# Attention with a token mixer: in the ending, the values of two steps are multiplied in one burst

## The chip, the cores and the metric

The kernel runs on one core of a Trainium2 chip. The time is the device time of that core in microseconds, the median of several runs. The engines are TensorE (PE in the profile; PEld is its loading of weights, PEq its sequencer), VectorE (DVE), ScalarE (ACT), GpSimd (POOL) and SyncE (SP), which issues most of the DMAs; each works through its own instructions in order. PSUM is the memory that PE writes: eight banks of 128 x 512 float32.

## The reference

Cut to what matters; x is 2048 tokens of 512 channels, and the sizes are 32 heads of 16 and a mixer of width 1792.

```python
xn = layernorm(x)
qkv = xn @ wqkv                                   # 32 heads of 16
p = softmax(einsum("qd,kd->qk", q, k) * 16 ** -0.5)
s = concat_heads(einsum("qk,kd->qd", p, v)) @ wo
h = layernorm(xn)
u = gelu(einsum("sd,sf->df", h, w1) + b1)
g = silu(einsum("df,fs->sd", u, w2) + b2)         # with the axes put back
return x + s * g
```

## The kernel before

**Steps.** After norms and projections, attention goes by pairs of heads: 16 pairs, each in 32 steps, 512 in all. A step t is one pair of heads, one span of 1024 queries and one block of 128 keys: 16 steps (key blocks) for the first span of a pair, 16 for the second. In a step `score` (L961) makes four tiles of scores, for two heads (a = 0, 1) and two halves of the queries. Each is a matmul of 50 rows, on the upper half of the PE array for a = 0 and on the lower for a = 1, so that the two can run side by side; ScalarE's exponential (L973) turns each into a tile `prob`.

`values` (L975) multiplies the four `prob` tiles of a step with the values of its 128 keys: four matmuls (L984), each 128 rows high and 32 columns wide, side by side, summed over the 16 steps of a span in one PSUM tile `av`. The pool of that tile has one bank. At the first step of a span `values` takes a new tile there. At the last step it puts `put_away` (L709) on the list `soon`, which copies `av` out; `run_later` (L507) records what is on that list. The code records instructions in Python's order and every engine gets its own in that order, with semaphores from the tile framework: a new tile in a bank waits until the old tile's last reader is done, also where that reader is recorded later on another engine.

**The main loop** (L1200) takes s = 0, 2, ..., 534 and treats two steps a turn. Up to s = 510 it also computes the row maxima for the steps 22 ahead (L525, L529). From s = 512 (`NU`) none are left; this is the ending. There t = s - 22, and the turn makes the scores of t (i = 0) and t + 1 (i = 1). Per i:

- `a_half` (L1145) records the four scores, interleaved with half-height matmuls of the output product (L1161). Products come from the generator `rest` (L1002 to L1030), three per block of 128 tokens; each is cut into an upper and a lower half. The upper halves are recorded at once, the lower ones two calls later (`second_rows`). With the lower halves the block is complete, and `finish` (L942) is recorded: VectorE multiplies by the gate (L944), adds (L945), SyncE stores the rows (L947), and `load_out` (L931) issues the loads for the third block after it (L938, L940). For s below 524 only i = 0 takes products, from 524 on both do. I call the matmuls of one call a series, and number the blocks 0 to 13 in the order of `blocks` (tokens' blocks 8 to 13, then 0 to 7); tokens' block 0 is number 6.
- one entry of `asides` is recorded, if there is one: `one` (L816: PE transposes L821, VectorE's reciprocals L824 and a copy L826) and `move_in` (L851: matmuls L835, L841, L842, L94, and four DMAs L98). They treat the first span of the last pair of heads, which ends with step 495; its copy is L714. Products of tokens' block 0 and after wait for `move_in`, by `own_done`, four calls of `run_later` later.
- `values` of the steps that are due.

**PSUM.** Before the ending four banks are for scores and sums of products, three for maxima, one for `av`. At s = 512 the seven become one rotation (L1211), from which scores, product blocks (for as long as they are summed) and the asides take tiles in turn.

**After the loop** eight loads of gates (`load_gates`, L956, on POOL's queue; six are recorded at s = 532, two behind the loop) go to buffers of `prob` tiles. Behind the last step's `values` (511), `put_away` copies the tile on ScalarE (L716); then follow products of the last two blocks (L1299), `one` and `two` for the second span (L821, L824, L826, L835), and the eight blocks of the second span are multiplied by their gates and stored (L1328, L1332, L1333).

Of the kernel before, what the change touches and what calls it, by code (L numbers as in the profile page):

```python
# [21 lines left out]
def tile_attention_token_mixer(ctx, tc, x, wqkv, wo, w1, b1, w2, b2, out):  # L22
# [484 lines left out]
    def run_later():  # L507
        now, later[:] = soon + later, []
        soon.clear()
        for f in now:  # L510
            f()

    NU = NP * NB * 2
    mxp = {}

    def max_of(u, half, a, pl=ps_mx, nm="mx"):

        p, r = divmod(u // 2, NB)
        c = u % 2 * 2 + half
        if u // 16 not in mxp:  # L520
            mxp[u // 16] = sm.tile([P, 2, 8, NC], F32, name="mxp")
        q, k = qs[p], ks[p]
        o = 64 * a
        ps = pl.tile([P, 512], F32, name=nm)
        nc.tensor.matmul(  # L525
            ps, q[o : o + 48, r * P : (r + 1) * P], k[o : o + 48, c * 512 : (c + 1) * 512],
            start=True, stop=True,
        )
        nc.vector.tensor_reduce(mxp[u // 16][:, a, r % 8, c : c + 1], ps, axis=AX.X, op=OP.max)  # L529
# [272 lines left out]
    def divisions():  # L802

        if undivided and undivided[0] in away and begun_divisions[0] - len(divided) < 2:
            divide(begun_divisions[0], *undivided.pop(0))
            begun_divisions[0] += 1
# [114 lines left out]
    def load_second():  # L921

        b = next((b for b in unkept if b >= PARTS), min(unkept))
        unkept.remove(b)
        i = b - NB // 2
        while not held or len(held) < NB // 8:
            held.append(big.tile([P, S], F32, name="big"))
        ys[b] = held[i // 4][:, i % 4 * 512 : i % 4 * 512 + 512]
        nc.sync.dma_start(ys[b], y_d[b] if b < PARTS else xv[:, b, :])
# [45 lines left out]
    def values(t):  # L975
        p, r = divmod(t, SPP)
        span, kb = divmod(r, NB)
        if kb == 0:
            state["av"] = ps_av.tile([P, 512], F32, name="av")
        av = state["av"]  # L980
        for a in range(2):
            for c in range(2):
                j = 2 * a + c
                nc.tensor.matmul(  # L984
                    av[32 * j : 32 * j + 32, :],
                    vps[p][:, kb, 16 * a : 16 * a + 32], prob.pop((t, a, c)),
                    start=kb == 0, stop=kb == NB - 1,
                )
        if kb == NB - 1:
            soon.append(lambda: put_away(p, span, av))  # L990
# [70 lines left out]
    def take(n, each):  # L1061

        nonlocal open_, done
        got = 0
        while open_ and (got < n or fill.peek() and len(fill.peek()) == 2):
            x = fill.next()
            if x is False:
                open_ = False
            elif x is None:
                break  # L1070
            elif len(x) == 2:
                def then(empty, back):
                    empty()
                    back()

                each(None, lambda x=x: then(*x))
                if fill.peek() is None:
                    fill.next()
                    break
            else:  # L1080
                each(x, None)
                got += 1
        done += got
# [20 lines left out]
    def order(n):  # L1104

        return ORDERS[min(x for x in ORDERS if x >= n)]

    def halves(lead, n):


        parts, then = ([], []), []

        def each(x, f):
            if f:
                then.append(f)
                return
            ps, w, m, first, last = x
            for a, made in ((lead, parts[0]), (1 - lead, parts[1])):
                r = slice(64 * a, 64 * a + 64)
                made.append(lambda r=r, start=first and a == lead, stop=last and a != lead: nc.tensor.matmul(  # L1120
                    ps, w(r), m(r), start=start, stop=stop,
                ))

        take(n, each)
        return *parts, then
# [3 lines left out]
    def count():  # L1129


        left = -done
        for i, n in enumerate(sizes):
            left += n
            if left > 0:
                break
        if left == 9:
            return 4
        return min(6, -(-left // -(-3 * left // (15 if i == SLOW else 16)))) if left > 0 else 0
# [35 lines left out]
    def items(s, a):  # L1175

        mx, sc = [], []
        for i in range(4):
            t = s - LEAD + i // 2
            if s < NU:  # L1180
                mx.append(lambda i=i: max_of(s + i // 2, i % 2, a))
            if 0 <= t < NT:
                sc.append(lambda t=t, i=i, at=(ps_mx, "mx") if a and s >= NU else (ps_sc, "sc"): score(t, i % 2, a, *at))
        return mx, sc
# [8 lines left out]
    def piece():  # L1193
        if pieces:
            pieces.pop(0)()
            return True
        return False

    lead = 0
    for s in range(0, total + 1, 2):  # L1200
        t = s - LEAD
        now[0] = s
        if s >= NU or t < 0:
            run_later()
        if done >= n_fill // 2 + 3 * NF:
            divisions()
        if s >= NU - SPP + LEAD and unkept:
            load_second()
        if s == NU:

            ps_sc.free += ps_mx.free  # L1211
            ps_mx.free = ps_sc.free
        heads = [items(s, a) for a in range(2)]
        if s < NU and t >= 0:
            steady[0] = True
            one, two, then = halves(lead, count())
            made = [dict(D=part, m=heads[a][0], s=heads[a][1]) for part, a in ((one, lead), (two, 1 - lead))]
            first, second, *places = order(len(one))
            if one:
                lead = 1 - lead  # L1220
            for i, kinds in enumerate((*zip(first, second), "")):
                if i in places:

                    if i == places[0]:
                        piece()
                    now[0] = s + places.index(i)
                    if now[0] >= LEAD + 2:
                        values(now[0] - LEAD - 2)
                    run_later()
                for of, kind in zip(made, kinds):  # L1230
                    if of[kind]:
                        of[kind].pop(0)()
            for f in then:
                f()
        elif s < NU:

            for i in range(4):
                for a in range(2):
                    max_of(s + i // 2, i % 2, a, *first_banks[n_max % 4])
                    n_max += 1  # L1240
                end = i == 3 and s + 2 == LEAD
                some = []
                take(EARLY[n_max // 2 % len(EARLY)], lambda *x: some.append(x))
                for x in some:
                    lanes(*x, stop=end and x is some[-1])
                if end:
                    keep_half()
                if i == 1:
                    now[0] = s + 1
                    run_later()  # L1250
        else:


            for i in range(2):

                a_half(*(heads[a][1][2 * i : 2 * i + 2] for a in range(2)), i == 0 or s >= NU + 2 * (PARTS - NB // 2))
                if not piece() and asides and s < total - 2:
                    asides.pop(0)()
                for v in range(t - 2, t + i):
                    if (v, 0, 0) in prob:  # L1260
                        values(v)
                if i == 0:
                    now[0] = s + 1
                    run_later()
            if s == NU + 4:
                load_last_w()
            if s == total - 2:
                load_gates(NB // 2, NB - 2)
            if s == total - 6:
                split_last_w()  # L1270
        if s < NU and s % 16 == 14:
            pieces[:0] = max_rows(s + 1)
        while t < 0 and piece():
            pass
        for v in (t - 2, t - 1):
            if 0 <= v < NT and (v, 0, 0) in prob:
                values(v)
        if 0 <= t < NT:
            p, r = divmod(t, SPP)
            if r == 0 and p + 1 < NP:  # L1280
                if p > 0:
                    load_qk(p + 1)
                load_v(p + 1)
# [101 lines left out]
```

## Time and profile before

| | |
|---|---|
| median of 3 runs | 1630.51 us (1629.91 to 1630.63) |
| span of the profiled execution | 1628.0 us |
| the profiled execution's own time beside its span | not given by the page |
| busy: PE, DVE, ACT, POOL | 1621.3, 1421.3, 1194.1, 564.1 us |
| the ending, 1563.14 to 1610.13 | 46.99 us |
| behind the last values, 1610.13 to 1628.0 | 17.87 us |

The span runs from the first to the last instruction that the profiler recorded; the time measured from outside also holds what lies around it. Busy times overlap. A busy PE is not PE at its peak: the ends of matmuls are modelled. In rows of the timeline stand the start, the duration, the engine, the line, the operation, the tiles (output<-inputs), their sizes and the number of instructions merged into the row; in brackets how long the engine had been idle, and what ended that.

### The profile page before, as it was taken

Reading aid. Unit: us, or ns where it says so; the run is one execution under the profiler, and the core shown is the slowest. Engines: PE = TensorE matmul, PEld = TensorE weight load, DVE = VectorE, ACT = ScalarE, POOL = GpSimd, SP = SyncE. Lnnn points to the kernel's source line nnn. Section 1 sums busy time; section 2 is a strip of 40 time slices with the busy share of each in tenths; the row PEclk is TensorE's granted clock in tenths of the full one; section 3 lists DMA queues with packets and bytes.
Section 4 is the critical chain, followed back from the end, with each engine's and each line's share of the span. In section 5 each row is a group of like instructions: output and inputs, shape, how many; then the busy total and the mean of one; then the engine's idle time right before and its main releaser. Section 6 shows DMA issues by size and latency. Waiting matters only on the chain.

```text
span 1628.0 us, 31317 instructions
## 1 busy us (share of the span) xinstructions
PE 1621.3 (100%) x11956; PEld 881.9 (54%) x11956; DVE 1421.3 (87%) x2497; ACT 1194.1 (73%) x2313; POOL 564.1 (35%) x672
## 2 busy tenths in 40 slices
PE   9999999999999999999999999999999999999998
PEld 8888855544555544545545545445555455454444
DVE  7665999999999999999999999999999999999955
ACT  3333477777777777777877777777777778888885
POOL 1224844342244432342333332322322224632342
PEclk9999999999999999999999999999999999999999
DMA  7468441514142141916151512314151615353356
GB/s 238 181 237 207 113 89 40 95 43 73 41 72 70 33 79 34 247 62 111 38 86 37 95 55 42 74 28 68 37 85 37 112 38 101 118 95 121 110 156 223
DMA packets 151810, 155.60 MB, mean 96 GB/s; under 512 B 51612, under 2 KB 109980, under 8 KB 148588
## 3 DMA queue, kind: packets, MB, share of 16 engines
q1 hardware_dynamic: 146604, 150.75, 38.2%
q0 software_dynamic: 5056, 2.85, 0.7%
q8 instruction: 94, 1.54, 0.4%
q14 instruction: 56, 0.46, 0.1%
HBM read 101.86 MB, written 50.58 MB: 94 GB/s over the span
## 4 chain that ended last, share of the span: by engine, by line
PE 99%; DVE 0%; DMA 0%; ACT 0%; SPq 0%; issue 0%
PE av L984 31%; PE dn L1120 24%; PE sc L968 18%; PE mx L525 13%; PE sc L428 3%; PE mx L428 2%; PE dn L663 2%; PE av L428 1%; PE dn L664 1%; PE sc L101 0%; PE sc L103 0%; PE sc L102 0%; PE dn L1161 0%; PE dn L1299 0%; PE mx L101 0%; PE mx L103 0%
## 5 line engine op out<-in xcount | busy, mean ns | idle before, releaser
L529 DVE TENSOR_REDUCE mxp<-mx 128x1 f32<-128x512 f32 x2026 | 1250.4, 681 | 120.6 <-PE mx L525 94.0
L973 ACT ACTIVATE prob<-sc 128x512 f32<-128x512 f32 x2004 | 1042.3, 606 | 288.9 <-PE sc L968 128.2
L525 PE MATMUL mx<-big 48*128 48x512 f32 x2026 | 764.8, 416 | 0.0
L968 PE MATMUL sc<-big 50*128 50x512 f32 x2004 | 738.1, 411 | 0.1
L984 PE MATMUL av<-prob,vp 128*32 128x512 f32 x4096 | 545.5, 604 | 0.0
L1120 PE MATMUL dn<-hu,wh 64*128 64x512 f32 x1520 | 514.7, 406 | 0.0
L968 PEld LDWEIGHTS sc<-big 50*128 50x128 f32 x2004 | 356.6, 186 | 254.3 <-ACT prob L973 230.2
L525 PEld LDWEIGHTS mx<-big 48*128 48x128 f32 x2026 | 358.2, 185 | 175.1 <-DVE mxp L529 156.9
L1120 PEld LDWEIGHTS dn<-hu,wh 64*128 64x128 f32 x1520 | 271.5, 184 | 74.9 <-issue 49.8
L1120 PE MATMUL dn<-hu,wl 64*128 64x512 f32 x762 | 302.4, 397 | 0.0
L984 PEld LDWEIGHTS av<-prob,vp 128*32 128x32 f32 x4096 | 80.9, 108 | 181.3 <-issue 169.6
L94 POOL TENSOR_TENSOR wl<-raw,wh 128x512 fp32r<-128x512 f32 x124 | 150.8, 1217 | 60.1 <-ACT wh L166 20.5
L1120 PEld LDWEIGHTS dn<-hu,wl 64*128 64x128 f32 x762 | 140.6, 184 | 12.9
L164 POOL CAST wh<-raw 128x512 fp32r<-128x512 f32 x104 | 60.4, 581 | 183.5 <-DMA raw<-in_B_w_dram 77.3
L552 POOL CAST m<-f 16x128 fp32r<-16x128 f32 x32 | 9.0, 280 | 302.1 <-DVE f L541 302.1
L98 POOL DMA_DIRECT2D big<-m x128 | 66.1, 525 | 2.7 <-PE mx L968 2.7
L613 POOL TENSOR_TENSOR sq<-u 128x512 f32<-128x512 f32 x11 | 11.4, 1041 | 132.8 <-ACT u L607 132.7
L700 POOL TENSOR_SCALAR t<-t 128x512 f32<-128x512 f32 x16 | 23.8, 1488 | 95.7 <-ACT t L697 95.7
L1120 PE MATMUL dn<-wh,hu 64*128 64x512 f32 x168 | 55.0, 393 | 0.0
L428 PE MATMUL sc<-xt,big 128*128 128x512 f32 x184 | 44.3, 389 | 0.0
L94 POOL TENSOR_TENSOR hu<-hx,hu 128x512 fp32r<-128x512 f32 x16 | 20.3, 1289 | 66.9 <-ACT hu L271 66.9
L663 PE MATMUL dn<-hu,wh 64*128 64x512 f32 x128 | 42.3, 391 | 0.0
(228 smaller groups left out, 1221.6 us busy)
## 6 DMA issues: line engine op xcount, KB each, us to landing
raw<-in_B_w_dram SPq DMA_DIRECT2D x104, 256.0 KB
big<-k_d SPq DMA_DIRECT2D x96, 128.0 KB
big<-q_d SPq DMA_DIRECT2D x96, 128.0 KB
q_d<-sg SPq DMA_DIRECT2D x16, 512.0 KB
k_d<-sg SPq DMA_DIRECT2D x16, 512.0 KB
num_d<-ev SPq DMA_DIRECT2D x30, 256.0 KB
u_d<-uo SPq DMA_DIRECT2D x14, 512.0 KB
hu<-u_d SPq DMA_DIRECT2D x14, 512.0 KB
```

The lines of the kernel that those rows point to most:

```text
L94: eng.tensor_tensor(out=o, in0=a, in1=b.bitcast(F32), op=OP.subtract)
L98: queue.dma_start(dst.bitcast(F32), src.bitcast(F32))
L164: nc.gpsimd.tensor_copy(whs[n][:, :m, :], raws[n][:, :m, :])
L428: nc.tensor.matmul(ps, w[part][:, kd, m], xt[kd][:, z, :], start=w is wh and z == 0 and kd == 0, stop=w is wl and kd == ND - 1,)
L525: nc.tensor.matmul(ps, q[o : o + 48, r * P : (r + 1) * P], k[o : o + 48, c * 512 : (c + 1) * 512], start=True, stop=True,)
L529: nc.vector.tensor_reduce(mxp[u // 16][:, a, r % 8, c : c + 1], ps, axis=AX.X, op=OP.max)
L663: nc.tensor.matmul(ps, w(slice(0, 64)), m(slice(0, 64)), start=first, stop=last)
L700: nc.gpsimd.tensor_scalar(t, t, 1.0, None, op0=OP.add)
L968: nc.tensor.matmul(ps, ks[p][o : o + 50, kb * P : (kb + 1) * P], qs[p][o : o + 50, at : at + 512], start=True, stop=True,)
L973: nc.scalar.activation(e, ps, AF.Exp, scale=scale)
L984: nc.tensor.matmul(av[32 * j : 32 * j + 32, :], vps[p][:, kb, 16 * a : 16 * a + 32], prob.pop((t, a, c)), start=kb == 0, stop=kb == NB - 1,)
L1120: made.append(lambda r=r, start=first and a == lead, stop=last and a != lead: nc.tensor.matmul(ps, w(r), m(r), start=start, stop=stop,))
```

## The change

In the ending the call of `values` at i = 0 is left out, save at s = 512. What was due there is called at i = 1 of the same turn, whose range covers it already.

```diff
@@ -1256,7 +1256,7 @@
                 a_half(*(heads[a][1][2 * i : 2 * i + 2] for a in range(2)), i == 0 or s >= NU + 2 * (PARTS - NB // 2))
                 if not piece() and asides and s < total - 2:
                     asides.pop(0)()
-                for v in range(t - 2, t + i):
+                for v in range(t - 2, t + i) if i or s == NU else ():
                     if (v, 0, 0) in prob:
                         values(v)
                 if i == 0:
```

Before, the order on PE from s = 514 on is: scores of t, values of t - 1, scores of t + 1, values of t. After, it is: scores of t, scores of t + 1, values of t - 1 and of t. As t is even there, a span's last step (495) and the next span's first (496) fall into one burst; `put_away` of 495 is then recorded after the matmuls of 496, and waits of the framework keep 496 behind the copy. Since `put_away` is recorded a series later, so are the asides that it appends. The last step (511) is multiplied at i = 1 of s = 534 instead of i = 0.

## The prediction

> **What bounds the kernel now.** I read the page first: the span, then the chain that ended last, which is the tensor engine almost alone.
>
> ```profile
> span 1628.0 us, 31317 instructions
> ...
> PE 99%; DVE 0%; DMA 0%; ACT 0%; SPq 0%; issue 0%
> ```
>
> The edit acts only where no maxima are left (s = 514 to 534), so next I read the timeline from 1558 us on, engine by engine. I count pairs of steps by s. Of PE, the columns are start, duration, engine, line, tiles, count; a `values` burst of one step shows as x8, because each of its four matmuls leaves two records.
>
> ```profile
> 1559.63 1.92 PE L984 MATMUL av<-prob,vp 128*32 128x512 f32 x16
> 1561.48 0.49 PE L968 MATMUL sc<-big 50*128 50x512 f32 x1
> ...
> 1563.14 0.49 PE L968 MATMUL sc<-big 50*128 50x512 f32 x1
> 1563.48 0.39 PE L968 MATMUL sc<-big 50*128 50x512 f32 x1
> 1563.71 0.40 PE L1161 MATMUL dn<-wh,hu 64*128 64x512 f32 x2
> ...
> 1564.50 1.06 PE L984 MATMUL av<-prob,vp 128*32 128x512 f32 x8
> 1565.50 0.50 PE L968 MATMUL sc<-big 50*128 50x512 f32 x1
> ...
> 1566.16 1.07 PE L984 MATMUL av<-prob,vp 128*32 128x512 f32 x8
> 1567.15 0.49 PE L968 MATMUL sc<-big 50*128 50x512 f32 x1
> ```
>
> This is the pair s = 514, 4.01 us: a row-tiled series with three products (five slots, two half-height matmuls side by side in each) 1.36, a burst 1.00, a series of scores alone (two slots) 0.66, a burst 0.99. Inside a series a slot is 0.23 (1563.48 to 1563.71); the first costs 0.34. The one double burst of today, s = 512, takes 1.85 instead of 2.00.
>
> **What joining saves.** Ten pairs (s = 514 to 532) lose one burst. Two joined series take 1.36 + 2 x 0.23 = 1.82 instead of 2.02, where only the first holds products, and 1.36 + 5 x 0.23 = 2.51 instead of 2.72, where both do. With 0.15 for the bursts that is 0.35 for a pair in which nothing waits.
>
> The Trainium skill, "TensorEngine Tiling (Array Packing)", section "Key Properties", says that changing the tiling mode drains the engine. By that rule each join saves one round trip between modes, ten times 0.35, and the sum would end at -3.5; the 0.34 first slots agree with it, but the rule is silent on what the joined series then waits for.
>
> **What the joined series waits for.** PE may write a score only when its PSUM bank is free. After s = 512 the four score banks and three maximum banks are one rotation of seven. Each open product block holds one, and one more is with VectorE (L944). In the built order, with both series filled, score 4+k of a pair takes the bank of score k of the same pair, so it waits for that exponential; today a 1.00 us burst lies between them. ScalarE's rows give the speed.
>
> ```profile
> 1594.64 0.50 PE L968 MATMUL sc<-big 50*128 50x512 f32 x1
> 1595.18 1.09 ACT L973 ACTIVATE prob<-sc 128x512 f32<-128x512 f32 x2 [0.29 <-PE dn L1161]
> 1596.15 1.10 ACT L973 ACTIVATE prob<-mx 128x512 f32<-128x512 f32 x2
> 1599.37 0.50 PE L968 MATMUL sc<-big 50*128 50x512 f32 x1
> ...
> 1608.01 1.09 ACT L973 ACTIVATE prob<-mx 128x512 f32<-128x512 f32 x2
> 1609.16 0.14 PEld L984 LDWEIGHTS av<-prob,vp 128*32 128x32 f32 x2 [0.34 <-ACT prob L973]
> ```
>
> The first exponential starts 0.54 after the first score; two take 0.97, so 0.485 apart, each 1.09 - 0.485 = 0.605 long. The fourth ends at 0.54 + 3 x 0.485 + 0.605 = 2.60. After an exponential's end (1609.10) PE loads weights 0.06 later; that burst ended at 1610.13 (row below), and one strip runs 1.85 - 1.00 = 0.85, so the matmul began near 1609.28: 0.18 after the release. The last score starts at 2.78, the burst at 3.11 (0.33, the last slot of a series), and the pair takes 3.11 + 1.85 = 4.96 against 4.73 today (1594.64 to 1599.37): **+0.23** instead of -0.35. If one more bank were free, the last score would wait for the third exponential and the pair would win 0.25; I take +0.23, as the built order names the fourth.
>
> Where only the first series holds products (s = 514, 516, 518, 522), the last two scores wait for the second exponential and for the L944 that reads the block just finished:
>
> ```profile
> 1564.00 1.12 ACT L973 ACTIVATE prob<-sc 128x512 f32<-128x512 f32 x2
> 1564.14 0.69 DVE L944 TENSOR_TENSOR gt<-dn,gt 128x512 f32<-128x512 f32 x1 [2.99 <-PE dn L1161]
> ```
>
> L944 starts 1.00 after the series, ends at 1.69, PE goes on at 1.87, the burst begins at 2.20: 4.05, or +0.03 (s = 516, 522). At s = 514 ScalarE is still behind (0.86 instead of 0.54), the second exponential ends at 1.95, the burst begins at 2.46: +0.30.
>
> **The boundary inside a burst.** Pair s = 518 multiplies steps 495 and 496, and 495 ends a query span. There is one accumulator bank; 496 may start only after L714 has copied it. Today the next scores cover that copy; joined, nothing does. The copy also feeds L821, which turns it for the division; L821 now comes one series later.
>
> ```profile
> 1571.17 0.49 PE L968 MATMUL sc<-big 50*128 50x512 f32 x1
> ...
> 1573.52 0.50 PE L968 MATMUL sc<-big 50*128 50x512 f32 x1
> 1573.69 0.69 DVE L714 COPY ev<-av 128x512 f32<-128x512 f32 x1
> 1574.53 0.63 PE L821 MATMUL mx<-ident,ev 128*128 128x128 f32 x4 [0.27 <-DVE ev L714]
> 1575.50 0.43 DVE L826 COPY t<-rq 128x512 f32<-128x512 f32 x1
> 1576.08 0.49 PE L968 MATMUL sc<-big 50*128 50x512 f32 x1
> 1577.08 0.69 DVE L944 TENSOR_TENSOR sq<-dn,sq 128x512 f32<-128x512 f32 x1 [1.15 <-PE dn L1161]
> 1577.44 1.16 PE L835 MATMUL mx<-ident,t 128*128 128x128 f32 x8
> 1577.81 0.69 DVE L945 TENSOR_TENSOR big<-big,sq 128x512 f32<-128x512 f32 x1
> 1578.53 1.06 PE L984 MATMUL av<-prob,vp 128*32 128x512 f32 x8
> 1581.19 0.50 PE L968 MATMUL sc<-big 50*128 50x512 f32 x1
> ```
>
> At s = 518: series to 2.20, burst 1.00, copy (0.17 to start, 0.69, 0.15 to restart) 1.01, burst 1.00: 5.21 against 4.91 (1571.17 to 1576.08, with L821 in it): +0.30. At s = 520 the order of VectorE changes too: L944 and L945 now stand ahead of the reciprocals (L824, L826) that L835 needs. Counted from the end of the first series, L944 starts at -0.36 (1577.08 against 1577.44), L945 ends at 1.06, L826 0.77 later (as from the end of L821, 1575.16, to 1575.93), PE restarts 0.15 after: 1.98, while PE's own work there (L821 0.63, series 0.66) is done at 1.29. The pair: 1.36 + 1.98 + 1.09 (L835) + 1.85 = 6.28 against 5.11: **+1.17**.
>
> **The end of the products.** The move-in behind L835 is one `run_later` later, so the products of block 6 (tokens' block 0, today from the first series of s = 524) begin one series later. Pair 524 has 14 half-matmuls instead of 17, about 2.2 + 1.85 against some 4.73: -0.6 (an estimate). The last three half-products fall behind the last double burst:
>
> ```profile
> 1604.09 0.49 PE L968 MATMUL sc<-big 50*128 50x512 f32 x1
> ...
> 1607.81 2.40 PE L984 MATMUL av<-prob,vp 128*32 128x512 f32 x16
> ...
> 1610.13 0.50 PE L1299 MATMUL dn<-wh,hu 128*128 128x512 f32 x1
> ```
>
> Today 6.04. Afterwards: series 2.8 (between 2.51 and 3.11, as the second lacks three halves), burst 1.85, three halves alone 0.34 + 0.23 + 0.33 = 0.90, step 511 1.00: 6.55, +0.5.
>
> **PE's sum:** +0.30 (514) +0.03 (516) +0.30 (518) +1.17 (520) +0.03 (522) -0.6 (524) +0.69 (526, 528, 530) +0.5 = **+2.4**. Step 511 ends near 1612.55.
>
> **What is late next.** The tail's reciprocals L824 stand on VectorE behind the last block's L944, and that waited for its gate:
>
> ```profile
> 1595.61 0.42 SPq L940 DMA_DIRECT2D gt<-g_d  x1
> ...
> 1600.38 0.69 DVE L944 TENSOR_TENSOR gt<-dn,gt 128x512 f32<-128x512 f32 x1 [0.94 <-PE dn L1161]
> 1602.83 0.45 SPq L940 DMA_DIRECT2D sq<-g_d  x1
> 1610.12 0.69 DVE L944 TENSOR_TENSOR sq<-dn,sq 128x512 f32<-128x512 f32 x1 [3.02 <-DMA sq<-g_d]
> 1611.81 0.28 DVE L824 RECIPROCAL rq<-sc 128x8 f32<-128x8 f32 x2 [0.27 <-PE sc L821]
> ...
> 1602.36 1.12 POOL L956 DMA_DIRECT2D prob<-g_d  x2 [30.27 <-PE dn L1161]
> ```
>
> The load of 1602.83 is issued once block 10 is finished, whose L944 is the row of 1600.38 (1.01 into pair 530), and takes 7.29. Today L824 has 0.23 of slack (0.73 for each of L944, L945: 1611.58). In the changed order block 10 ends a series later, in the second half of pair 530, behind block 9's L944 and L945 and the split of the last weights: 1.01 + 3 x 0.73 = 3.20 into a pair that starts 1.69 later (the sum up to 528): 1604.26, **+3.88**. The load then lands at 1614.00, L824 runs at 1615.46 instead of the 1614.23 that PE would allow: +3.65 in all. From L824 on PE waits for VectorE and the tail (17.87 from 1610.13 to the span's end) is unchanged. So the span becomes 1631.65; the page gives no separate time of the profiled execution, and the median lies 2.51 above the span, which I carry over: 1630.51 + 3.65 = **1634.2**.
>
> **Rivals.** Each is judged by 0.2% of the time, 3.26 us, about what a measurement of this kernel tells from no change.
> (a) The load sets the end, +3.65: chance 0.55, of which 0.13 falls below +3.26, since a pair's few tenths decide.
> (b) The load lands in time, because the eight gate loads of L956 that compete with it come at other moments; PE's sum is left: +2.4, 1632.9. For it: block 10's gate, issued at 1595.61, was there 4.77 later (its row names PE, not a DMA). Against: the last one took 7.29. Chance 0.20, 0.03 of it above the bound.
> (c) The load lands still later: today two gate loads precede it (1602.36), in the changed order six come together once step 508 is multiplied, some 0.53 apart, around 1605 to 1608. Up to 1.5 more, as three that now follow it would go ahead of it, at POOL's 0.53 apiece: +5.1, 1635.6. Chance 0.15.
> (d) Banks do not bind, but the boundary does: six pairs at -0.35, 518 and 520 +1.1, 524 -0.6, the end +0.2: -1.4 on PE. Block 10 comes 3.20 - 1.01 = 2.19 later in a pair that starts 1.25 earlier, and 0.23 is slack: L824 holds the end at +0.7, 1631.2. Chance 0.07.
> (e) Nothing waits at all: ten joins, -3.5, 1627.0. For it, PE fills 99% of the chain; against it, ScalarE's 0.485 x 8 = 3.88 a pair leaves 0.13 under today's 4.01. Chance 0.03, the only faster one.
>
> Slower by over 0.2%: 0.42 + 0.03 + 0.15 = 0.60. Within: 0.13 + 0.17 + 0.07 = 0.37. Faster: 0.03. The range leaves out (d), (e) and the ends of (b) and (c): 1631.5 to 1635.8.
>
> **What would show it.** Right: L984 in ten groups of x16 with about 1.85 each, one split near its middle by L714 for 1.0; PE or its weight loads waiting for ACT L973 in the joined series of s = 526 to 530 (pairs near 4.95); L835 waiting for L826; the last L944 waiting for DMA, and L824 right behind L945 instead of after L821. Wrong: pairs of 4.4 there (banks free), or L824 released by PE L821 (then +2.4 at most), or no wait at the boundary.

## The result, and the profile after

| | before | after |
|---|---|---|
| median | 1630.11 us (12 runs, 1629.53 to 1631.12) | 1634.35 us (12 runs, 1632.41 to 1636.77) |
| profiled execution, own time / span | not given / 1628.0 us | 1634.56 / 1632.8 us |

The changed kernel is slower by 4.24 us, ratio 1.0025 (95% interval 1.0018 to 1.0033). Its runs are spread 4.4 us wide, those of the kernel before 1.6.

From the page of the changed kernel, the span, and the chain that ended last by engine:

```profile
span 1632.8 us, 31313 instructions
...
PE 97%; DVE 1%; DMA 1%; ACT 0%; issue 0%; SPq 0%; DVEq 0%
```

PE had 99% of the chain, VectorE and the DMAs 0% each; now these two have 1% each and PE 97%. So the chain now makes a detour over a transfer, and the timeline has to show where. First PE's own part, up to step 511, in the timeline of the changed kernel (start, duration, engine, line, tiles, sizes, count, and in brackets the idle time before and what ended it). Three stretches: the pair s = 514, the boundary with s = 518 and 520, and the pair s = 530.

```profile
1563.16 0.49 PE L968 MATMUL sc<-big 50*128 50x512 f32 x1
...
1565.62 1.92 PE L984 MATMUL av<-prob,vp 128*32 128x512 f32 x16
1567.47 0.49 PE L968 MATMUL sc<-big 50*128 50x512 f32 x1
...
1571.50 0.49 PE L968 MATMUL sc<-big 50*128 50x512 f32 x1
...
1573.73 1.06 PE L984 MATMUL av<-prob,vp 128*32 128x512 f32 x8
1574.87 0.69 DVE L714 COPY ev<-av 128x512 f32<-128x512 f32 x1 [0.88 <-PE av L984]
1575.61 1.07 PE L984 MATMUL av<-prob,vp 128*32 128x512 f32 x8 [0.81 <-DVE ev L714]
1576.61 0.49 PE L968 MATMUL sc<-big 50*128 50x512 f32 x1
...
1577.61 0.69 DVE L944 TENSOR_TENSOR sq<-dn,sq 128x512 f32<-128x512 f32 x1 [2.05 <-PE dn L1161]
...
1578.94 0.27 DVE L824 RECIPROCAL rq<-mx 128x8 f32<-128x8 f32 x2
1579.25 0.43 DVE L826 COPY t<-rq 128x512 f32<-128x512 f32 x1
1579.82 1.13 PE L835 MATMUL mx<-ident,t 128*128 128x128 f32 x8 [0.54 <-ACT prob L973]
1580.88 1.92 PE L984 MATMUL av<-prob,vp 128*32 128x512 f32 x16
1582.73 0.49 PE L968 MATMUL sc<-big 50*128 50x512 f32 x1
...
1600.81 0.49 PE L968 MATMUL sc<-big 50*128 50x512 f32 x1
...
1602.48 0.50 PE L968 MATMUL sc<-big 50*128 50x512 f32 x1 [0.25 <-ACT prob L973]
...
1603.91 1.92 PE L984 MATMUL av<-prob,vp 128*32 128x512 f32 x16
1605.77 0.49 PE L968 MATMUL sc<-big 50*128 50x512 f32 x1
...
1612.29 0.50 PE L1299 MATMUL dn<-wh,hu 128*128 128x512 f32 x1
```

A pair's time is the distance from its first score to that of the next pair: 1563.16 to 1567.47 is s = 514. All of them, with the change that was predicted for each:

| pair s | before | after | change | predicted |
|---|---|---|---|---|
| 514 | 4.01 | 4.31 | +0.30 | +0.30 |
| 516, 522 | 4.02, 4.01 | 4.03, 4.03 | +0.01, +0.02 | +0.03 each |
| 518 | 4.91 | 5.11 | +0.20 | +0.30 |
| 520 | 5.11 | 6.12 | +1.01 | +1.17 |
| 524 | 4.72 | 4.19 | -0.53 | -0.6 |
| 526, 528, 530 | 4.72, 4.73, 4.72 | 4.93, 4.93, 4.96 | +0.21, +0.20, +0.24 | +0.23 each |
| 532 to L1299 | 6.04 | 6.52 | +0.48 | +0.5 |

L1299 begins at 1612.29 instead of 1610.13: **+2.16** on PE (0.02 of it before s = 514). The other half comes behind it. Same timeline, the loads and the multiplications by the gates:

```profile
1603.25 0.34 SPq L947 DMA_DIRECT2D out_dram<-u  x1
...
1603.74 0.68 DVE L944 TENSOR_TENSOR gt<-dn,gt 128x512 f32<-128x512 f32 x1
...
1605.54 3.23 POOL L956 DMA_DIRECT2D prob<-g_d  x6 [33.54 <-ACT prob L973]
...
1606.28 0.32 SPq L938 DMA_DIRECT2D u<-y_d  x1
1606.65 0.48 SPq L940 DMA_DIRECT2D sq<-g_d  x1
...
1615.22 0.69 DVE L944 TENSOR_TENSOR sq<-dn,sq 128x512 f32<-128x512 f32 x1 [5.05 <-DMA sq<-g_d]
1615.95 0.69 DVE L945 TENSOR_TENSOR u<-u,sq 128x512 f32<-128x512 f32 x1
1616.56 0.27 DVE L824 RECIPROCAL rq<-sc 128x8 f32<-128x8 f32 x2
...
1617.15 1.16 PE L835 MATMUL sc<-ident,t 128*128 128x128 f32 x8 [2.52 <-DVE t L826]
```

The last block's gate load is issued at 1606.65 instead of 1602.83 and takes 8.57 us instead of 7.29. VectorE, in order, holds L824 behind that block until 1616.56 instead of 1611.81, **+4.75**, and PE stands for 2.52 us before L835. The whole loss of the profiled execution (span +4.8) is in these two numbers: 2.16 of PE, and 2.59 more of a load.

The issue is late in two steps. L944 of block 10 (1603.74, before 1600.38) comes 3.36 us later. Then SyncE has to issue the row load of the last block first (L938, 1606.28), and that waits until the store of block 9's rows, which uses the same tile (L947, 1603.25), has landed: 0.7 us of waiting in the profile after, 0.2 in the one before. The prediction does not have this second step.

### The profile page after: what moved, and what is told of

Its sections match the earlier page's. It is cut to its first block, busy times and chain, and to the rows that moved or that the text cites. A ratio compares the mean times of both kernels' runs of the same rounds, so it can differ in the third digit from the quotient of the medians.

```text
span 1632.8 us, 31313 instructions
## 1 busy us (share of the span) xinstructions
PE 1621.9 (99%) x11956; PEld 885.4 (54%) x11956; DVE 1420.8 (87%) x2497; ACT 1193.1 (73%) x2313; POOL 564.2 (35%) x672
## 4 chain that ended last, share of the span: by engine, by line
PE 97%; DVE 1%; DMA 1%; ACT 0%; issue 0%; SPq 0%; DVEq 0%
PE av L984 31%; PE dn L1120 23%; PE sc L968 17%; PE mx L525 14%; PE sc L428 3%; PE mx L428 2%; PE dn L663 2%; PE av L428 1%; PE dn L664 1%; DMA sq<-g_d 1%; PE sc L101 0%; PE sc L103 0%; PE sc L102 0%; PE dn L1161 0%; PE mx L103 0%; PE mx L101 0%
```

## The experiments

The ending does not begin at the same time in all executions: the double burst of s = 512 lies at 1559.63 in the profile before, at 1559.2 to 1560.8 in the others. So I give positions in a trace as a distance from that burst, which I call the mark. Before, L1299 begins 50.50 behind the mark and L824 52.18; after (mark 1559.65), 52.64 and 56.91. Medians are compared with the runs of the kernel before on the same chip: 1630.38 us for experiments 1 to 4, 1630.36 for 6 and 8 to 10, 1629.92 for 5, 7 and 11, 1630.66 for 12.

**1 and 2. The load out of the way, with and without the change.** The last block's two loads get buffers of their own and are issued at the beginning of the ending. `after_early_load` has this and the change, `before_early_load` this alone.

```diff
 def load_out(n):
...
+        if b in gts and n == len(blocks) - 1:
+            return
...
+        b = blocks[-1]
+        ys[b] = el.tile([P, D], F32, name="y_last", bufs=1)
+        nc.sync.dma_start(ys[b], y_d[b])
+        last_g = el.tile([P, D], F32, name="g_last", bufs=1)
+        nc.sync.dma_start(last_g, g_d[b])
...
+        gts[b] = last_g
```

> The changed kernel, with the last block's two loads (rows to add, gate) in buffers of their own and issued at s = 512, so that nothing in the tail waits for them. If the late load sets the end, only PE's loss is left: the last L944 waits for PE and not for a DMA, L824 follows L821, and the time is +2.2 over before (PE's loss in the profile of the changed kernel, 2.16), 1632.3. If the load is innocent and the tail is late for another reason (the eight gate loads, the copy of the last values), the time stays at +4.2, 1634.3. Its spread over the runs should shrink to that of before if the load makes the spread.

> The same two early loads in the kernel before. There L824 has 0.23 us of slack behind the last L944, so the theory of the late load expects 0 (within 0.4). If early loads help by themselves (less on the queues at the end), it is faster by 1 or more, and the gain of the run with the changed kernel would not be the load's lateness.

Measured: 1633.00 us (10 runs, 1632.48 to 1634.13), ratio 1.0016 (1.0007 to 1.0026), against 1630.97 without the change, ratio 1.0002 (0.9993 to 1.0011). From the timeline of the changed kernel with early loads (its lines are up to eight further down: L946 is L944):

```profile
1612.27 0.69 DVE L946 TENSOR_TENSOR g_last<-dn,g_last 128x512 f32<-128x512 f32 x1 [1.28 <-PE dn L1169]
...
1614.83 0.28 DVE L824 RECIPROCAL rq<-sc 128x8 f32<-128x8 f32 x2 [1.14 <-PE sc L821]
```

VectorE is idle ahead of L824 and waits for PE: the load is off the path. With the mark at 1560.46, L824 is 54.37 behind it, +2.19; with the early loads alone it is where it was, at 52.18 (1613.01, mark 1560.83). Between the two medians lie 2.03 us. So PE's part is 2.0 to 2.2, as its timeline said, and the rest of the 4.24 is the load. With it gone the runs are spread 1.65 us wide instead of 4.4: the spread came with the load too. (The early loads alone came out 0.59 above the kernel before, where I had allowed 0.4; that is within what a measurement can tell, and in the trace none of it lies in the ending.) Both kernels begin the ending 0.8 to 1.2 us later than the profile before; why stays open, and for that I compare them with one another.

**3 and 4. The boundary pair.** `split518` leaves s = 518 in two bursts and joins the other nine; `only518` joins that one alone.

```diff
-for v in range(t - 2, t + i) if i or s == NU else ():
+for v in range(t - 2, t + i) if i or s in (NU, NU + 6) else ():
```

and, for the second,

```diff
-for v in range(t - 2, t + i) if i or s == NU else ():
+for v in range(t - 2, t + i) if i or s != NU + 6 else ():
```

> The change, but pair s = 518 keeps its two bursts, so that no burst spans the two query spans, the move-in is not late and the products start where they do today. The nine other pairs are joined. If the boundary and what it makes late is the cause: PE loses 0.3 (514) + 0.65 (526 to 530) and wins 0.5 in the last pairs, in all +0.3 to +0.6, the load is late by no more than that, and the time is +0.5, 1630.6. If the waits for banks in the nine joined pairs are the main cost, it stays at +2 or more, 1632.1. If joins win as such, it is at -3, 1627.

> Only pair s = 518 is joined, all others keep two bursts. By the boundary theory PE loses 0.2 at 518, 0.6 at 520 (L821 moves there; L835 now stands behind a burst, which covers VectorE), and 0.55 at the end, where three half-products stand alone: +1.35; block 10 is finished in the second series of pair 530, +3.2 later, so the load sets the end at about +3, 1633.1. If the banks are the main cost, one pair costs +0.2 to +0.5, 1630.5.

Measured: nine pairs without the boundary 1631.03 us (1630.45 to 1631.49), ratio 1.0004 (0.9995 to 1.0014), +0.65. The boundary pair alone 1635.34 us (5 runs, 1634.56 to 1639.33), ratio 1.0034 (1.002 to 1.0047), +4.96. By the medians one pair costs what ten cost, though with five runs its interval is wide (3.3 to 7.7 us). From the timeline of the kernel that joins s = 518 alone:

```profile
1576.16 1.06 PE L984 MATMUL av<-prob,vp 128*32 128x512 f32 x8 [0.81 <-DVE ev L714]
...
1606.82 0.64 SPq L940 DMA_DIRECT2D sq<-g_d  x1
...
1615.12 0.69 DVE L944 TENSOR_TENSOR sq<-dn,sq 128x512 f32<-128x512 f32 x1 [2.78 <-DMA sq<-g_d]
...
1616.45 0.27 DVE L824 RECIPROCAL rq<-sc 128x8 f32<-128x8 f32 x2
```

With the mark at 1560.27, L1299 is 1.58 later than before and L824 4.0. The load is issued 46.55 behind the mark, before 43.20. What delays it is not the sum of PE's waits, but that the asides, recorded a series later, push the products of block 6 and all after it a series back. In the kernel with nine pairs the load is in time. It takes 4.25 us, and VectorE then waits for PE ahead of L824:

```profile
1604.78 0.46 SPq L940 DMA_DIRECT2D sq<-g_d  x1
...
1605.39 3.23 POOL L956 DMA_DIRECT2D prob<-g_d  x6 [32.02 <-ACT prob L973]
...
1609.03 0.69 DVE L944 TENSOR_TENSOR sq<-dn,sq 128x512 f32<-128x512 f32 x1 [0.40 <-DMA sq<-g_d]
...
1612.87 0.28 DVE L824 RECIPROCAL rq<-sc 128x8 f32<-128x8 f32 x2 [2.42 <-PE sc L821]
```

My expectation for the single pair, +3, was too small by 2 in the median and by 1 in the trace (L824 +4.0). PE's 1.58 came near the 1.35 that I had said, and the issue came 3.35 later where I had said 3.2; the load took 8.30 us instead of 7.29. The parts do not add up (0.65 and 4.96 make more than 4.24). PE's small losses can vanish while everything waits for the load, but the excess is also within the interval of the five runs; which it is stays open.

The trace of the nine pairs holds something else. Two of its joins win: s = 520, where the matmuls of L835 stand between the two series, takes 4.97 instead of 5.11. And s = 532, the last, takes 5.58 up to L1299 instead of 6.04: its two series take 2.52 instead of 2.73, its three bursts 3.06 instead of 3.31. The others lose it again: s = 514 (+0.31), 522 (+0.20) and 526 to 530 (+0.21 each), so that L1299 is 0.52 later. In the changed kernel neither gain shows (+1.01 and +0.48 in the table), as the boundary moves other work into both pairs.

**5. The boundary pair with the load out of the way.** `only518_early`: the edit of `only518` and the early loads.

> Only pair s = 518 joined, with the last block's two loads in buffers of their own and early, as in the run after_early_load. If in the run only518 (+5.0) PE lost 1.6 and the late load the rest, the tail's L824 now follows L821 and the time is 1.6 above the kernel before with the same early loads (1630.97): 1632.5. If the load does not matter, it stays near 1635.3.

Measured: 1631.64 us (1631.04 to 1632.34), ratio 1.0011 (1.0001 to 1.0021): 3.70 below the kernel without early loads, 1.72 above the kernel before, 0.67 above `before_early_load`, which ran on another chip (I had expected 1.6). In its trace L1299's counterpart is 52.05 behind the mark (+1.55) and L824 53.83 (+1.65). So of the boundary pair's 4.96, some 1.7 are PE's and 3.2 to 3.7 the load's.

**6 and 7. Pairs of one kind alone.** `only526` joins s = 526, 528, 530; `only514` joins s = 514, 516, 522.

```diff
-for v in range(t - 2, t + i) if i or s == NU else ():
+for v in range(t - 2, t + i) if i or not NU + 14 <= s <= NU + 18 else ():
```

```diff
-for v in range(t - 2, t + i) if i or s == NU else ():
+for v in range(t - 2, t + i) if i or s not in (NU + 2, NU + 4, NU + 10) else ():
```

> Only the pairs s = 526, 528 and 530 are joined, those with products in both series; no query span ends there, and nothing else moves. By the theory of the banks each takes 4.95 us instead of 4.73, as the fourth exponential of a pair releases its last score: +0.65, and the time is +0.4 to +0.7, 1630.9. If the banks are free, each join saves 0.35 and the time is -1.05, 1629.3.

> Only the pairs s = 514, 516 and 522 are joined, which have products in the first series alone. By the waits for ScalarE (514) and for L944 (516, 522) they take 4.31, 4.05 and 4.05 us instead of 4.01: +0.35 in all, and the time is +0.3, 1630.7. If the joins win as such: -1.05, 1629.3.

Measured: 1631.06 us (1630.37 to 1631.63), +0.70, ratio 1.0003 (0.9993 to 1.0012), pairs of 4.94, 4.93 and 4.94; and 1630.45 us (1629.95 to 1631.83), +0.53, ratio 1.0003 (0.9994 to 1.0012), with L1299 51.05 behind the mark (+0.55) and pairs of 4.33, 4.05 and 4.26. Each median by itself is within what a measurement can tell; the traces carry the reading. The 4.26 of s = 522 is a miss: I had expected 4.05. There the weight loads of the second series wait for exponentials and not for L944. None of these pairs wins: where both series hold products a join costs 0.2, where one does it costs 0.0 to 0.3.

**8 and 9. Half the exponentials.** From s = 514 on, `short_exp_before` and `short_exp_after` compute the exponentials of 256 of the 512 columns only, and the products read those twice.

```diff
-        nc.scalar.activation(e, ps, AF.Exp, scale=scale)
+        if now[0] < NU + 2:
+            nc.scalar.activation(e, ps, AF.Exp, scale=scale)
+            return
+        nc.scalar.activation(e[:, :256], ps[:, :256], AF.Exp, scale=scale)
+        prob[t, a, c] = e[:, :256].unsqueeze(1).to_broadcast([P, 2, 256])
```

> The kernel before with half the exponentials in the ending left out: from the second step of s = 512 on ScalarE does 256 of 512 columns, and the product with the values reads those twice, so PE's work is as before. ScalarE is not what bounds the two bursts of today: pairs s = 526 to 530 stay at 4.73; only the stall of 0.5 before the last burst goes.

> The changed kernel with the same half of the exponentials left out. If the joined pairs wait for ScalarE to free their banks, exponentials of about 0.4 free them in time (the fourth ends near 1.85, and the last score is due at 2.2): pairs s = 526 to 530 fall from 4.95 to 4.40, below the 4.73 of two bursts. If they wait for anything else (modes of the array, products, weights), they stay near 4.95. The pair s = 516, which waits for L944, stays near 4.03 in both.

Measured: 1629.98 us without the change, ratio 0.9995 (0.9985 to 1.0006), and 1633.97 with it, ratio 1.002 (1.001 to 1.0031). Without it the pairs stay at 4.72: ScalarE did not bound them. With it, s = 526 falls from 4.93 to 4.38: the wait was for exponentials, and with that wait gone the join wins 0.34, the saving that the prediction had worked out. In the same way s = 514 falls from 4.31 to 4.03, while s = 516 stays at 4.04, as its wait is for L944. But s = 528 and 530 fell only to 4.76 and 4.73, where I expected 4.40. From the loads of weights in the timeline of that kernel (its exponential is L976):

```profile
1597.10 0.18 PEld L968 LDWEIGHTS sc<-big 50*128 50x128 f32 x1 [0.27 <-ACT prob L976]
...
1597.60 0.18 PEld L968 LDWEIGHTS sc<-big 50*128 50x128 f32 x1 [0.31 <-DVE sq L944]
...
1602.33 0.18 PEld L968 LDWEIGHTS sc<-big 50*128 50x128 f32 x1 [0.24 <-DVE sq L944]
```

The second wait is for L944: a bank of the second series is that of the block finished in the first, and VectorE has it until it has multiplied. Shorter exponentials only uncover that next reader. The time of the whole, 4.0 above, hardly moved, as the load still sets the end (its L944 waited 5.05 us for the DMA).

**10. The burst in the other place.** `burst_i0` joins the two steps of a span: at i = 0 those of t - 2 and t - 1, so that no burst spans the boundary.

```diff
-for v in range(t - 2, t + i) if i or s == NU else ():
+for v in range(t - 2, t) if i == 0 else ():
```

> Joined at i = 0 instead of i = 1: a burst takes steps t - 2 and t - 1, an even and the odd one after it, so it never spans two query spans, and the copy of step 495, the move-in and the products come when they do in the kernel before (s = 512 is joined so too). By the boundary theory the copy is covered, and only the banks cost: PE within -1 to +1, the last load late by as much as PE, the time within 1 of before, 1630.6. If joining is dear wherever the burst stands, +2 or more, 1632.5.

Measured: 1633.37 us (1633.0 to 1634.55), ratio 1.0017 (1.0008 to 1.0026), +3.0; I had expected no more than 1 either way. From PE's timeline of that kernel:

```profile
1564.50 1.92 PE L984 MATMUL av<-prob,vp 128*32 128x512 f32 x16
...
1566.36 0.49 PE L968 MATMUL sc<-big 50*128 50x512 f32 x1
...
1567.54 0.50 PE L968 MATMUL sc<-big 50*128 50x512 f32 x1 [0.22 <-ACT prob L973]
...
1568.94 1.92 PE L984 MATMUL av<-prob,vp 128*32 128x512 f32 x16
1570.80 0.49 PE L968 MATMUL sc<-big 50*128 50x512 f32 x1
```

There the series without products comes first, the second begins 1.18 us after the first score (1566.36 to 1567.54) and waits for a bank: this pair takes 4.44 (to 1570.80), the others of the kind up to 4.50, instead of 4.01. L1299 is 2.96 later, and L824 follows PE (`PE sc L821` released it), not the load. So "the boundary costs, the banks are small" was too narrow: a join costs 0.4 to 0.5 where the series without products comes first, and 0.0 to 0.3 where it comes second.

**11. All gate loads recorded behind the loop.** `after_late_gates`: the changed kernel, with the six loads L956 of s = 532 moved to the other two.

```diff
-            if s == total - 2:
-                load_gates(NB // 2, NB - 2)
...
-    load_gates(NB - 2, NB)
+    load_gates(NB // 2, NB)
```

> The changed kernel, but all eight gate loads of POOL's queue are recorded behind the loop, so that they are issued only when the last products are done and no longer run beside the last block's load. If that load is late because the six gate loads that now come together run beside it (8.6 us to land instead of 7.3), it lands in about 5 us, before PE is done with step 511, L824 follows L821, and the time is +2.2, 1632.5, provided the gates themselves are there for the tail. If it is late only because it is issued 3.8 us later, the time is +3.5 or more, 1633.9.

Measured: 1634.04 us (6 runs, 1632.82 to 1637.42), ratio 1.0028 (1.0017 to 1.004). From its timeline:

```profile
1605.56 3.23 POOL L956 DMA_DIRECT2D prob<-g_d  x6 [32.87 <-ACT prob L973]
...
1606.53 0.50 SPq L940 DMA_DIRECT2D sq<-g_d  x1
...
1613.47 0.69 DVE L944 TENSOR_TENSOR sq<-dn,sq 128x512 f32<-128x512 f32 x1 [3.32 <-DMA sq<-g_d]
```

The edit moved nothing: GpSimd issues the six at 1605.56 instead of 1605.54, as they wait for their buffers and not for their place in the list (both rows name an exponential as what ended the wait). So it tells nothing of the theory, but something else: with the same loads issued at nearly the same moments the same load took 6.94 us here and 8.57 above.

**12. The six gate loads behind the last load.** `six_behind`: the same six on SyncE's queue.

```diff
-            nc.gpsimd.dma_start(gates[b], g_d[b])
+            (nc.sync if hi < NB else nc.gpsimd).dma_start(gates[b], g_d[b])
```

> The changed kernel, with the six gate loads that it issues together on GpSimd's queue (1605.54, 1.1 us ahead of the last block's gate load of 1606.65) recorded on SyncE's queue instead, where they stand behind that load and behind the next-to-last store, so that they start some 4 us after it. If the six loads are what makes that load take 8.57 us instead of the 7.29 of before, it lands in under 7.3 us, the reciprocals L824 run by 1615.3 or earlier (counted for a start of the ending at 1559.65), and, unless the six themselves come too late for the multiplications at the very end, the time is 1633 or less. If the load's time has nothing to do with them, it takes 7 to 8.6 us as in the changed kernel, and the time stays at 1634 or above.

Measured: 1634.11 us (11 runs, 1633.46 to 1636.83), ratio 1.0022 (1.0013 to 1.0031). From its timeline:

```profile
1606.84 0.48 SPq L940 DMA_DIRECT2D sq<-g_d  x1
...
1611.27 3.74 SPq L956 DMA_DIRECT2D prob<-g_d  x6
1612.09 0.69 DVE L944 TENSOR_TENSOR sq<-dn,sq 128x512 f32<-128x512 f32 x1 [1.30 <-PE dn L1161]
...
1614.64 0.28 DVE L824 RECIPROCAL rq<-sc 128x8 f32<-128x8 f32 x2 [1.14 <-PE sc L821]
...
1620.17 0.69 DVE L1328 TENSOR_TENSOR prob<-sc,prob 128x512 f32<-128x512 f32 x1 [1.52 <-DMA prob<-g_d]
```

The load now takes 5.25 us at most (PE, not the DMA, releases L944), and L824, 54.39 behind the mark (1560.25), has only PE's +2.21 left. So without gate loads in front it is shorter: 8.57 with the six, of which about three start ahead of it (they come 0.53 apart, the first 1.1 us ahead), 5.25 at most with all of them behind. One execution could be chance, as the 6.94 shows, but the other traces say the same. Where no gate load starts ahead of it, it takes 4.25 (the nine pairs), at most 4.56 (`only526`) and at most 5.25. Where some do, it takes 6.59 (`burst_i0`), 6.94, 7.29 (before), 8.30 (`only518`), 8.57 and 8.59 (`short_exp_after`). What one such load adds is no fixed number. The time is the same all the same: the six come too late for the last multiplications, VectorE waits 1.52 us for one of them (L1328), so the delay of the loads is paid at another place. No version with joined pairs was faster than the kernel before.

## Why the prediction came out right

1634.2 was predicted and 1634.35 measured, slower, inside the range. Its likeliest case, (a), is what the trace shows, with a part of (c). The direction and the mechanism were foreseen; that the two times lie only 0.15 apart is luck, as the points below show.

- **What joining saves and what it waits for.** Right in kind and in size: +0.30, +0.03 and +0.23 were predicted, +0.30, +0.01 to +0.02 and +0.20 to +0.24 measured. That the exponentials bind at s = 526 is shown by experiment 8/9 (4.93 to 4.38), that L944's bank is next behind them too. Rival (e), ten joins with no wait and -3.5, fell: in the changed kernel no pair came out shorter, except s = 524, whose products moved on. Rival (d) fell with the pairs of 4.93, and rival (b) with the 5.05 us that L944 waited for the load. The rule of the Trainium skill that stands beside it ("TensorEngine Tiling (Array Packing)", section "Key Properties": a change of tiling mode drains the engine) is not contradicted, as the double bursts do take 1.85 (1565.62 to 1567.47 above) and not 2.00; what the joined series waits for is more than it saves.
- **The boundary.** Right in mechanism, a little dear: the copy stops PE for 0.88 (1.88 from one burst's start to the other's, less 1.00), not 1.01, as PE restarts 0.05 after L714 and not 0.15. At s = 520 PE restarts 1.86 after the series (1577.96, by the start of L821, to 1579.82) instead of 1.98. There I said that L835 waits for L826; the profile names the exponential. L826 ends at 1579.68 and PE goes on at 1579.82; an exponential of the second series (start 1579.08, 0.61 long) ends at 1579.69, and this trace cannot tell which of the two it would have been without the other. The kernel with half the exponentials can: there that exponential ends 0.22 before L826, and PE still goes on 0.14 after L826 and 1.86 after the series. So L826 alone is enough, as predicted.
- **PE's sum.** +2.16 for +2.4; s = 518 and 520 came 0.26 cheaper, the rest is hundredths.
- **What is late next.** The issue of the last load was predicted 3.88 later and came 3.82 later, but by two errors that cancel. The prediction has it follow block 10 at a fixed distance; block 10's L944 came 3.36 later and not 3.88, and the wait for block 9's store, which the prediction does not have, made up the rest. The term that was mis-sized is the load's duration: I kept 7.29, and it was 8.57 in the profiled execution, so that L824 came +4.75 and not +3.65. The reason is the one that rival (c) gave, gate loads that now start ahead of it; experiment 12 and the other traces bear it out. But its size is no fixed number, 6.94 in another execution with the same loads.
- **From the span to the median.** The prediction carried over 2.51 between the span before and the median shown, and the span came out at 1632.8 instead of 1631.65. After, the profiled execution's own time lies only 1.76 above its span. So the profile before was of an execution faster than its median, by about 0.75 if the same 1.76 lies around it, and this error and the too short load nearly cancelled. The change itself was +3.65 predicted and +4.24 measured between medians; the median before, 1630.51 of three runs, came out 0.40 lower with twelve, which hides most of that difference.
- **What I had not seen.** The ten joins are not alike: one of them, at the boundary, carries the whole load term. The prediction has the step (block 6 a series later), but did not say that without s = 518 the rest costs +0.65, within what a measurement can tell, nor that two of the joins (s = 520 and 532) then win.

## What to carry to other kernels

Joining two bursts of the engine that bounds a kernel saves a few tenths a time only where the next work on it waits for nothing; what stood between the bursts was the cover for other engines' releases of banks, and for a single accumulator it was the cover for its copy. Look then for what is recorded later because of the join: a list that slips by one place moved the last load by 3.8 us, and an in-order engine put work of the critical chain behind it. A load in a stretch in which the DMA engines are full has no duration to be read from one row; take a range, and see which other loads are in front.

## What the runs showed of the hardware

From the busy times by stretch, before and then after (columns: length; busy time of PE, PEld, DVE, ACT, POOL; PE's granted clock; share of the DMA engines; GB/s):

```profile
1604.00:1610.00 6.00, 6.00 (x42) 2.42 (x38) 2.14 (x4) 4.67 (x10) 3.19 (x6) 1.00 0.96 316
1610.00:1616.00 6.00, 6.00 (x31) 4.65 (x31) 5.02 (x18) 1.69 (x5) 0.11 (x1) 1.00 0.65 256
```

```profile
1604.00:1610.00 6.00, 6.00 (x49) 2.47 (x49) 4.27 (x7) 5.07 (x11) 3.23 (x6) 1.00 0.97 310
1610.00:1616.00 6.00, 4.63 (x30) 2.26 (x22) 0.92 (x3) 0.91 (x2) 1.06 (x2) 1.00 1.01 364
```

I had not expected the DMA engines to be full here (a share of 0.96 to 1.01), in a kernel whose page shows a mean of 95 GB/s. Before, they are full from 1604 to 1610 and have room when the tail begins; after, they are full to 1616, and a 256 KB load took between 4.25 and 8.59 us, the longer ones with gate loads started ahead of it. The changed kernel's runs differ by 4.4 us with such a load on the path, and by 1.65 with it out of the way (experiment 1).
